# A fused sparse-attention and MLP kernel: a shorter start chain, a seventh tracked PSUM bank, and an order of work taken from a search of the scheduling model

## The chip, the cores and the metric

The kernel runs on one core of a Trainium2 chip. The metric is the device time of one execution in microseconds (us). Most executions of one kernel agree within a few tenths of a per cent, some kernels here only within about one per cent, and medians are quoted. PSUM is the memory that matmuls write to, in eight banks here. PE is the matrix engine, PEld its weight loads, DVE the vector engine, ACT the scalar engine, POOL the general one, SP the engine that issues most DMA transfers here.

## The reference, cut to what matters

Block-sparse attention over 4 batches, 8 heads, 768 positions and a head size of 64, followed by a residual MLP of two steps, one across positions ("token" work) and one across channels:

```python
mask = |qb - kb| <= 1, or first / last block, or one of 3 sampled blocks per query block
attn = softmax(where(mask, q k^T / 8, -1e9)) v          # B=4, H=8, S=768, D=64
x    = attn rearranged to [B, 768, 512]
tok  = w_tok @ (alpha1 * x + beta1)                      # 768 x 768 over positions
u    = x + lam * tok
a2   = alpha2 * u + beta2
out  = u + lam * (relu(a2 @ w_ch1) @ w_ch2)              # 512 -> 2048 -> 512
```

Sixteen pairs of heads are worked off one after another. The first channel product (`uT`, `w1b`) fills a bank of PSUM, ACT or DVE applies the relu and writes a slice of the tile `hts`, and the second channel product (`w2b`, `hts`) reads four such slices at a time.

## The kernel before

The program has no fixed loop nest. It holds a list of jobs (engine, modelled duration, priority, buffers taken and given) and a model of the chip's time. The model walks through time, picks the next job for each engine, and so writes one fixed instruction order for every engine. The chip then runs that order. Where the model finds nothing for PE to do it puts in dummy matmuls (`fill`), which are instructions like any other: if the chip is later than the model, PE still has to run them. The parts that the change and the argument touch:

```python
def bank_order(tc, instructions, psum, nb):
    # for every instruction that touches the shared PSUM tile: which waits it really needs
    ...
        for kind in ("ins", "outs"):
            for a in getattr(ins, kind):
                ...
                if ap.tensor.name != psum:
                    names.add(ap.tensor.name)        # any other tile: by its name, as a whole
                    continue
                ...                                  # the shared PSUM tile: bank by bank
        if not banks:
            continue                                 # touches no bank: left to the usual tracking
        ...
        for n in names:
            for r in shared.get(n, ()):              # every earlier instruction that named it
                if r.engine != ins.engine or ins.engine != mybir.EngineType.PE:
                    real[r.name] = r                 # keep a dependency on it
            shared.setdefault(n, []).append(ins)
        tc.declare_no_dep(ins, group=psum, keep=list(real.values()), reason="other banks")
```

```python
ps6 = ps.tile([P, 6 * 512], FP, name="ps6", ...)     # six banks in one tile, handled by bank_order
BANKS = tuple(f"b{i}" for i in range(6))
...
wps = ps.tile([P, 512], FP, name="cp", tag="cp", bufs=1)   # a tile of its own: dummies and w2b products
keep_warm(9, 512)                                    # nine dummies before any data is there
...
# second channel product: into "cp" or "ops", both tiles of their own
cps[kk, mi] = bank(tag, [P, DM]) if tag in BANKS else ps.tile([P, DM], FP, name=tag, tag=tag, bufs=1)
for nk in range(4 * r, 4 * r + 4):
    nc.tensor.matmul(cps[kk, mi][:, 0:w], hts[kk][:, nk, ts(m, P)], w2tile[0][:, nk, lo : lo + w], ...)
...
T0 = 6600.0                                          # the model's time at which the list starts
```

The softmax here doesn't subtract the row's maximum and nothing guards it: scores larger than these inputs give would overflow.

## Time and profile before

| | before |
|---|---|
| time, median of 3 runs | 310.68 us (310.44 to 310.88) |
| span of the profiled execution | 308.2 us |
| first scores / first channel matmul / first `w2b` matmul | 7.72 / 59.70 / 72.05 us |
| last matmul | 304.45 us |
| clock of PE released | 6.4 us after the start |

The prediction below shows the main views. The waits of PE over the whole span (engine, line, what it waited for, then total us, times, longest) are two:

```profile
PE cp L236 <- DVE warm L231: 1.2, 1, 1.2
PE ps L716 <- ACT qx L303: 0.7, 1, 0.7
```

Both lie in the start. After it PE never waits long enough to be listed. The waits of ACT begin with the relu L1039:

```profile
ACT hts L1039 <- PE ps L1026: 36.4, 26, 9.6
```

In the timeline of SP's issues (start, length, kind) the mask goes out before any transpose of a head:

```profile
46.47 15.78 SPq L556 DMA_DIRECT2D maskT<-mask_rows  x18
62.55 1.32 SPq L657 DMA_TRANSPOSE qx<-rel  x1
```

### The profile page before, as it was taken

The numbers are of one execution on the slowest core, as the hardware profiler recorded it, in microseconds if no ns is written. First come the engines' busy times: TensorE is split into PE (matmuls) and PEld (weight loads), VectorE is DVE, ScalarE is ACT, GpSimd is POOL, SyncE is SP. The second block draws the span as 40 slices with busy tenths as digits, with TensorE's granted clock in tenths as the row PEclk, the third lists the DMA queues.
The fourth block names the chain that finished last, engine by engine and source line by source line (L and its number), as shares of the span: only waits on it lengthen the run. The fifth ranks groups of instructions, "written<-read, shape, count | busy, mean of one in ns | idle before, by whom it ended". The sixth has DMA issues, their size and how long they took to land.

```text
span 308.2 us, 7605 instructions
## 1 busy us (share of the span) xinstructions
PE 302.7 (98%) x3197; PEld 189.0 (61%) x3197; DVE 207.6 (67%) x434; ACT 206.3 (67%) x272; POOL 53.2 (17%) x91
## 2 busy tenths in 40 slices
PE   7999999999999999999999999999999999999995
PEld 3687788775656557555656557555656665555444
DVE  3699898879979788778759788778768730010111
ACT  4999998988676667577676666577658727428000
POOL 4656532001121121212021121120000000000000
PEclk9999999999999999999999999999999999999999
DMA  6999999993347634874444624983110110010121
GB/s 150 186 258 224 212 203 215 177 146 68 51 101 123 104 62 54 146 121 95 76 93 84 102 62 56 147 107 79 28 37 34 28 28 34 34 70 0 50 89 68
DMA packets 47210, 30.81 MB, mean 100 GB/s; under 512 B 27552, under 2 KB 43080, under 8 KB 47176
## 3 DMA queue, kind: packets, MB, share of 16 engines
q0 software_dynamic: 15984, 15.47, 32.0%
q1 hardware_dynamic: 30940, 14.61, 21.0%
q8 instruction: 25, 0.41, 0.6%
q10 hardware_dynamic: 252, 0.24, 0.2%
q14 instruction: 9, 0.07, 0.1%
HBM read 32.04 MB, written 6.33 MB: 124 GB/s over the span
## 4 chain that ended last, share of the span: by engine, by line
PE 76%; DMA 15%; issue 4%; POOL 3%; DVE 1%; POOLq 0%
PE ps L1026 26%; PE cp L1076 22%; DMA v<-in_v_dram 9%; PE ops L870 8%; PE ps L837 8%; PE ps L947 7%; PE ops L1076 5%; DMA k<-in_k_dram 3%; DMA wtk<-in_moe_w_tok_dram 3%; DMA q2f<-in_q_dram 1%; POOL q L383 1%; POOL k L383 1%; POOL w1b L448 1%; POOL v L383 0%; DVE x_sb L957 0%
## 5 line engine op out<-in xcount | busy, mean ns | idle before, releaser
L789 ACT ACTIVATE eT<-ps 128x1024 f16<-128x1024 f32 x90 | 87.0, 1023 | 29.4 <-PE ps L837 28.6
L1026 PE MATMUL ps<-uT,w1b 128*128 128x384 bf16 (+1 forms) x512 | 92.9, 326 | 0.1
L1039 ACT ACTIVATE hts<-ps,b1t 128x384 bf16<-128x384 f32 x106 | 61.4, 583 | 40.3 <-PE ps L1026 36.4
L1076 PE MATMUL cp<-w2b,hts 128*128 128x512 bf16 (+1 forms) x320 | 77.2, 374 | 0.0
L794 DVE TENSOR_TENSOR eT<-eT,maskT 128x1024 f16<-128x1024 f16 x90 | 60.6, 686 | 12.7 <-ACT eT L789 12.5
L1026 PEld LDWEIGHTS <-w1b 128*128 128x128 bf16 x512 | 46.9, 98 | 30.3 <-ACT eT L789 1.0
L1076 PEld LDWEIGHTS <-hts 128*128 128x128 bf16 x400 | 36.6, 98 | 36.4 <-issue 3.0
L731 ACT ACTIVATE eT<-ps 128x1024 f16<-128x1024 f32 (+1 forms) x55 | 52.4, 1020 | 3.4 <-PE ps L716 3.2
L870 PEld LDWEIGHTS <-eT 128*128 128x128 f16 x720 | 30.9, 97 | 15.7 <-issue 3.8
L947 PE MATMUL ps<-a1p,wtokT 128*128 128x128 bf16 x576 | 36.2, 219 | 0.0
L870 PE MATMUL ops<-vext,eT 128*128 128x65 f16 x720 | 35.8, 193 | 0.0
L947 PEld LDWEIGHTS <-wtokT 128*128 128x128 bf16 x576 | 32.9, 98 | 1.5 <-issue 0.6
L1093 DVE TENSOR_TENSOR ot<-x_sb,cp 128x512 f32<-128x512 f32 (+1 forms) x20 | 13.5, 673 | 28.4 <-PE cp L1076 28.3
L716 PE MATMUL ps<-qx,kx 88*128 88x512 bf16 (+1 forms) x144 | 31.7, 326 | 0.7 <-ACT qx L303 0.7
L381 POOL COPY held<-flag 1x1 bf16<-1x1 bf16 x24 | 10.5, 438 | 123.1 <-DVE flag L401 123.1
L837 PE MATMUL ps<-qx,kx 64*128 64x512 bf16 (+1 forms) x240 | 26.1, 326 | 0.0
L756 PEld LDWEIGHTS <-eT 128*128 128x128 f16 x432 | 18.2, 97 | 4.6 <-DVE x_sb L691 0.6
L756 PE MATMUL ops<-vext,eT 128*128 128x65 f16 x432 | 20.2, 193 | 0.0
L957 DVE TENSOR_TENSOR x_sb<-x_sb,ps 128x384 f32<-128x384 f32 x32 | 17.6, 550 | 3.5 <-PE ps L947 3.1
L691 DVE TENSOR_TENSOR x_sb<-ops,rcp 128x384 f32<-128x384 f32 x32 | 17.8, 558 | 1.1
L1093 DVE TENSOR_TENSOR ot<-x_sb,ops 128x512 f32<-128x512 f32 (+1 forms) x5 | 3.2, 635 | 22.5 <-PE ops L1076 22.5
L1043 DVE TENSOR_SCALAR hts<-ps,b1t 128x384 bf16<-128x384 f32 x22 | 13.6, 618 | 6.8 <-PE ps L1026 5.2
(69 smaller groups left out, 227.2 us busy)
## 6 DMA issues: line engine op xcount, KB each, us to landing
out_dram<-ot SPq DMA_DIRECT2D x23, 256.0 KB
v<-in_v_dram POOLq DMA_DIRECT2D x16, 192.0 KB, 4.4
q<-in_q_dram POOLq DMA_DIRECT2D x15, 192.0 KB, 4.7
k<-in_k_dram POOLq DMA_DIRECT2D x15, 192.0 KB, 3.5
w1b<-in_moe_w_ch_dram POOLq DMA_DIRECT2D x4, 512.0 KB, 9.9
w2b<-in_moe_w_ch_dram POOLq DMA_DIRECT2D x4, 512.0 KB, 15.0
wtk<-in_moe_w_tok_dram POOLq DMA_DIRECT2D x3, 384.0 KB, 9.6
maskT<-mask_rows SPq DMA_DIRECT2D x14, 72.0 KB
```

The costliest lines, as they stand in the source:

```text
L691: nc.vector.tensor_tensor(out=x_sb[:, s0 : s0 + NT, h * D : (h + 1) * D], in0=op[:, :, 0:D], in1=rcp[:].unsqueeze(2).broadcast_to([P, NT, D]),
L716: nc.tensor.matmul(sps[:, f - u * UN : f - u * UN + w], kx[h][0:KC, ts(jt, P)], qx[h][0:KC, c : c + w], start=True, stop=True,)
L731: nc.scalar.activation(eT[:, c], sps[:, c], AF.Exp, bias=EXPB, scale=SCALE)
L756: nc.tensor.matmul(ops[p, a][:, t * VW : t * VW + D + 1], eTs[p, u][:, ts(i - u * GU, P)], vx[:, a, jt, 0 : D + 1], start=(i % HT == 0), s ...
L789: nc.scalar.activation(eT[:], sps[:], AF.Exp, bias=EXPB, scale=SCALE)
L794: nc.vector.tensor_tensor(out=e, in0=e, in1=maskT[:, u, :].unsqueeze(1).broadcast_to([P, 2, 512]), op=ALU.min,)
L837: nc.tensor.matmul(sps[:, a * 512 + lo : a * 512 + lo + w], kx[sl][r, ts(jt, P)], qx[sl][r, c : c + w], start=True, stop=True,)
L870: nc.tensor.matmul(ops[p, a][:, t * VW : t * VW + D + 1], eTs[p, u][:, a * 512 + c * P : a * 512 + (c + 1) * P], vx[:, a, jt, 0 : D + 1], ...
L947: nc.tensor.matmul(tp[:, j, :], wtokT[:, s, ts(3 * g + j, P)], tl["a1p", p][:, s, :], start=(s == 0), stop=(s == NT - 1),)
L1026: nc.tensor.matmul(hp[:, 0:nc_], w1b[:, dk, ts(f, P)], uTs[b][:, dk, hf * HS : hf * HS + nc_], start=(dk == 0), stop=(dk == 3),)
L1039: nc.scalar.activation(hts[kk][:, f, :], hp[:, 0:HS], AF.Relu, bias=b1t[:, f : f + 1], scale=1.0)
L1076: nc.tensor.matmul(cps[kk, mi][:, 0:w], hts[kk][:, nk, ts(m, P)], w2tile[0][:, nk, lo : lo + w], start=(nk == 0), stop=(nk == 15),)
```

## The change

Its intent is to begin the scores a microsecond earlier, to give the order of work a seventh PSUM bank for single products, and to replace a hand-made order of loads and some priorities by one that a search found to be shorter in the scheduling model. Cut to its core:

```diff
-LEAD = 18
+LEADS = (14, 14, 14, 14, 29, 22, 28, 13, ...)        # one per pair
+PATS = (0.0, 0.0, 0.0, 0.0, 0.0, 1200.0, ...)        # how long a group waits for more units
+NUDGE = {(2, 26, 0): -3.0, ...}                       # priorities of five jobs
+LOADS = ("v 0", "q 1", "k 1", "a1", "tok 0", "k 2", "q 2", "q 4", "v 1", ...)
+PR = 0                                                # priority of DVE jobs of the fourth pair
+UTN = 3                                               # transposes of ub that leave PE for DMA
...
-    ps6 = ps.tile([P, 6 * 512], FP, name="ps6", tag="ps6", bufs=1)
+    ps6 = ps.tile([P, 7 * 512], FP, name="ps6", tag="ps6", bufs=1)
+    ALL = BANKS + ("b6",)              # b6 takes w2b products, dummies and some early scores
...
-    wps = ps.tile([P, 512], FP, name="cp", tag="cp", bufs=1)
-            nc.tensor.matmul(wps[:, 0:w], warm[:, 0:P], warm[:, 0:w], start=True, stop=True)
+            nc.tensor.matmul(bank(name, [P, w]), warm[:, 0:P], warm[:, 0:w], start=True, stop=True)
...
-    keep_warm(9, 512)
+    keep_warm(7, 512)
+    keep_warm(2, P)
...                                        # start chain: two small tables in one transfer, the mask
...                                        # product from kx[3], its scaling in the copies behind it
-    T0 = 6600.0
+T0 = 5600.0
...
-        if b == 0:
+        if b == 0 and n >= UTN:           # else: DMA transpose on SP
...
-                        cps[kk, mi] = bank(tag, [P, DM]) if tag in BANKS else ps.tile(...)
+                        cps[kk, mi] = bank(tag, [P, DM]) if tag in ALL else ps.tile(...)
...
-                take = ((("cp", "ops") + ...
+                take = ((("b6", "ops") + ...
...
-    bank_order(tc, list(nc.cur_bb.bb.instructions), ps6_name[0], len(BANKS))
+    bank_order(tc, list(nc.cur_bb.bb.instructions), ps6_name[0], len(ALL))
```

## The prediction

> **What bounds the kernel now.** I read the page's busy table first, then one table of five stretches of the span, then the order of instructions inside three of them.
>
> ```profile
> PE 302.7 (98%) x3197; PEld 189.0 (61%) x3197; DVE 207.6 (67%) x434; ACT 206.3 (67%) x272; POOL 53.2 (17%) x91
> ```
>
> PE (the matrix engine) is the bound, but 98% can't be taken as 98% useful: dummy matmuls on the tile `warm` keep it awake and count as busy. The stretches, chosen at the first scores (7.72), the first channel matmul of L1026 (59.70), the last token work and the last matmul (columns: length, then busy time and count on PE, weight loads, DVE, ACT, POOL, then clock, DMA share, GB/s):
>
> ```profile
> 0.00:7.72 7.72, 5.87 (x24) 2.47 (x25) 2.97 (x12) 3.21 (x5) 3.86 (x10) 1.00 0.64 150
> 7.72:59.70 51.98, 51.98 (x781) 40.40 (x782) 44.91 (x98) 49.36 (x55) 22.52 (x34) 1.00 1.18 213
> 59.70:254.50 194.80, 194.67 (x2114) 118.92 (x2113) 153.36 (x316) 135.14 (x181) 26.80 (x48) 1.00 0.48 82
> 254.50:304.45 49.95, 49.95 (x281) 27.21 (x278) 5.93 (x9) 18.59 (x32) 0.00 (x0) 1.00 0.13 48
> 304.45:308.20 3.75, 0.27 (x3) 0.00 (x0) 0.42 (x1) 0.00 (x0) 0.00 (x0) 0.81 0.17 57
> ```
>
> Five regimes. (1) 7.72 us before any score. (2) 52 us of attention: ACT is busy 49.36 of 51.98 with exps of about 1.03 us each, so ACT sets the pace and PE fills up with dummies. (3) 195 us in which attention and channel matmuls mix. (4) 50 us of channel matmuls alone. (5) A 3.75 us tail. In (3) and (4) PE never waits to speak of.
>
> The start-to-start distance of neighbouring matmuls says what PE really spends. Four channel matmuls take 0.65 us (L1026) or 0.86 us (L1076), 18 token matmuls 1.00 us. Around a group of paired scores (L837) there is more:
>
> ```profile
> 120.41 0.28 PE L870 MATMUL ops<-vext,eT 128*128 128x65 f16 x4
> 120.63 0.61 PE L837 MATMUL ps<-qx,kx 64*128 64x512 bf16 x6
> 121.17 1.04 PE L1076 MATMUL cp<-w2b,hts 128*128 128x512 bf16 x4
> ```
>
> The four L870 take 4 x 0.029 = 0.12 us, so L837 could start at 120.53 and starts at 120.63; its six matmuls run two at a time and need 2 x 0.216 = 0.43 us, and the next starts at 121.17, not 121.06. Over all 38 such groups I find 0.20 us a group, the same for groups of two units and of three: 38 x 0.204 = 7.8 us. Other distances above the usual sum to 0.3 us after 59.7. So the end is first scores + real PE work + dummies + group changes + tail; nothing else has room.
>
> The first scores hang on this chain:
>
> ```profile
> 1.19 4.02 PE L236 MATMUL cp<-warm 128*128 128x512 bf16 x9 [1.19 <-DVE warm L231]
> 2.60 1.28 ACT L277 ACT_TABLE_LOAD   x1 [2.60 <-issue]
> 3.89 0.51 ACT L277 CAST rel<-k2f 128x384 bf16<-128x384 f32 x1
> 5.01 0.85 PE L284 MATMUL ps<-identb,rel 128*128 128x128 bf16 x6
> 5.79 0.49 PE L294 MATMUL ps<-kx,mbb 24*24 24x384 bf16 x1
> 6.31 0.36 DVE L298 COPY kx<-ps 64x384 bf16<-64x384 bf16 x1 [1.20 <-PE ps L294]
> 7.21 0.47 ACT L303 CAST qx<-ops 24x384 bf16<-24x384 f32 x1
> 7.72 1.03 PE L716 MATMUL ps<-qx,kx 88*128 88x512 bf16 x5 [0.66 <-ACT qx L303]
> ```
>
> Two avoidable waits stand in it. The cast of k is over at 4.40, but nine cold dummies (0.427 us start to start) keep PE until 5.01. And the DVE copy into `kx` idles 1.20 us for L294, which reads other rows of the same tile.
>
> **What the Trainium skill says.** *Perfetto Trace Analysis*, Identifying the Most-Contended Engine, calls matmul busy share a poor measure of distance to the limit; this trace agrees, as PE is shown 98% busy with 11.4 us of dummies in it. *TensorE: Matmul & The Clock Gate*, What's actually happening, says that the array starts at half rate and is released after some 3.4 us of activity; here 128-column matmuls are 0.107 us apart at 5.0 to 5.5 us and 0.056 us apart from 6.56 us. *TensorEngine Tiling (Array Packing)*, Key Properties, says that a change of tiling mode drains the engine; the 0.20 us around each L837 group (64 rows against 128) fits, though other causes are not excluded. *DMA: Bandwidth & Descriptors*, DMA Transpose (X-bar), says the plain transpose is issued by Sync or ScalarE alone; the twelve transposes of `uT` on SP agree.
>
> **The change, part by part.**
> *Start.* Seven wide and two narrow dummies instead of nine: 7 x 0.427 + 2 x 0.107 = 3.20 us from 1.19, so PE is free at 4.39. One ACT-queue issue fewer (the 0.66 us `tab`) lets the table load and the cast of k go earlier; that cast then waits for k itself, which I put at 3.65, and ends at about 4.15. Transposes start at 4.4 instead of 5.01: -0.6 us. The mask product reads `kx[3]`, so the DVE copy no longer waits for it; the 0.38 us L261 goes, its arithmetic moving into the two copies that follow the product anyway. Walking on with the old durations: transposes to 5.05, products at 5.1 and 5.4, DVE copies to about 6.1, its mask rows to 6.7; ACT's mask rows by 6.4, and the last ACT copy (upper half of `kx`) is not needed by the first unit. First scores at about 6.75: **-0.95 us**.
>
> *Dummies and transposes in stage 2.* By the built order, dummies after the first scores go from 10,422 to 12,659 columns: at 2.4 columns a ns, 4.34 to 5.27 us, **+0.93 us**. Three of four batch-0 transposes of `ub` leave PE for DMA: 18 x 0.056 = **-1.0 us**. The two cancel; the first channel matmul comes again at the 48th unit of attention, as before. So stage 2 keeps its length of 52 us and only starts earlier. ACT has one 0.8 us copy fewer in it, but that can't help: the dummies are fixed instructions, and PE has to run them.
>
> *Groups.* The lead limits, the patience and the seventh bank change how paired scores are grouped: 24 of two units and 14 of three become 15 and 20. 38 to 35 groups: 3 x 0.204 = **-0.6 us**.
>
> *Rest.* All other matmuls keep their number and shape. Attention now ends nearer to the end (in the built order some 48 us of PE work follows the last token matmul, before 57), still enough to hide everything. The tail of 3.75 us stays.
>
> Sum: -0.95 + 0.93 - 1.0 - 0.6 = -1.6 us, from 310.7 to **309.1 us**.
>
> **The rivals.**
> A. *The order of loads misfits the chip.* Stage 2 moves 213 GB/s at a DMA share above 1, and the loads wait in one POOL queue. In the new order two of the `w1` slices come very late, after the v of five pairs, and three DMA transposes join the crowd. Order on PE is fixed, so a late load stops it. For it: the list was found in a model, not on the chip. Against: the old `w1` loads were issued by 28 us and needed at 59.7. Cost if true: 1 to 3 us, giving 310 to 312.
> B. *The mask becomes the wait.* On SP the third `uT` transpose now stands ahead of the 15.8 us of mask issues, which started at 46.5 and had the head transposes right behind them until 69.6. If that transpose waits until 51, the first paired scores move to about 74. The built order has moved them behind the first L1076 work, where I put 74; a miss costs 1 to 2 us.
> C. *The early start is swallowed*, because loads, not scores, pace stage 2: then only 0.5 us is won, 310.1. Against it: ACT runs its first sixteen exps with no gap.
> D. *The start and priorities are worth more*: if the three high-priority token steps of the fourth pair arrive early, PE still can't skip its dummies; the most I see is 1 us more, 308.
>
> **Range and chances.** The three gains are counted on the engine that is never idle, so I hold on to 309.1; a few tenths of error each way on the start, and A or B one time in four. Range 307.9 to 310.8. A gain over 2% needs 6.2 us, more than all the waits I can find outside the start; a loss over 2% needs a stall of 7 us. Faster 0.03, same 0.95, slower 0.02.
>
> **What would show it.** First scores at 6.6 to 7.0 us; first channel matmul at 58.2 to 59.2; 35 groups of paired scores at 0.20 us each; the last matmul at about 302.8, with the tail unchanged. The prediction is wrong if PE shows idle time or stretched matmul distances between 40 and 80 us (A by a wait for `w1b`, `v` or `uT`, B by one for `maskT`, `qx` or `kx`), or if the clock is released late because the shorter warm-up leaves a gap.

## More of the kernel before

Whatever an instruction reads outside the shared tile is known to `bank_order` only by name. The relu reads a bank of `ps6` and writes `hts`, so it is handled there. The second channel product wrote `cp`, so it was not.

## The result, and the profile after

The changed kernel is correct and slower: 320.73 us median of 4 runs (318.06 to 321.22), against 310.78 us for the kernel before in the same rounds. The ratio is 1.0304, with a 95% interval of 1.0245 to 1.0362. Ratios here and below are the mean time of one kernel's fast runs over that of the other's of the same rounds, so not quite the ratio of the medians quoted.

From the page after, the busy line and the clock line (tenths of full speed in 40 slices):

```profile
PE 308.4 (97%) x3185; PEld 190.9 (60%) x3185; DVE 206.0 (64%) x429; ACT 207.1 (65%) x273; POOL 53.3 (17%) x91
PEclk9999999799999999999999999999999999999999
```

Twelve matmuls fewer than before (18 transposes fewer, six dummies more), and yet 5.7 us more of busy time. Part of that is dummies, and part ran on a slower clock: the 7 in the eighth slice (56 to 64 us) shows it. The table by stage, cut at first scores, first channel matmul, first `w2b` matmul and last matmul (length, then busy time and count of PE, PEld, DVE, ACT, POOL, then clock, DMA share, GB/s):

```profile
0.00:7.54 7.54, 5.78 (x24) 2.70 (x25) 2.81 (x12) 3.22 (x5) 3.56 (x10) 1.00 0.63 152
7.54:66.92 59.38, 56.55 (x769) 41.87 (x769) 43.84 (x98) 48.88 (x54) 22.64 (x34) 0.97 1.15 195
66.92:85.27 18.35, 17.13 (x186) 11.50 (x184) 13.82 (x31) 13.18 (x26) 0.00 (x0) 1.00 0.54 110
85.27:315.80 230.53, 228.67 (x2207) 134.82 (x2208) 145.12 (x291) 141.78 (x189) 27.08 (x48) 1.00 0.40 71
```

The second stage took 59.38 us where it took 51.98 before, so the first channel matmul came 7.2 us late. The last two stages together took 248.88 us where 244.75 us stood before, another 4.1. PE has idle time in all of them now.

To see what the time went into, I split the start-to-start distances of all matmuls into useful work (at the usual distance for their width), dummies, and the rest, which holds waits, group changes and the slow clock:

| us | first scores | to first channel matmul: work, dummies, rest | from there to the last matmul: work, dummies, rest | last matmul |
|---|---|---|---|---|
| before | 7.72 | 46.39, 4.73, 0.86 | 235.52, 0, 9.22 | 304.45 |
| after | 7.54 | 45.39, 6.61, 7.38 | 235.53, 0, 13.36 | 315.80 |

So of 11.35 us, 0.18 was won in the start and 1.0 in transposes. Dummies took 1.9 more, the rest before the first channel matmul (waits and the slow clock) 6.5, and the rest after it 4.1. Three places carry it.

**The start.** PE's timeline:

```profile
1.19 3.38 PE L246 MATMUL ps<-warm 128*128 128x512 bf16 x9 [1.19 <-DVE warm L242]
4.94 0.80 PE L288 MATMUL ps<-identb,rel 128*128 128x128 bf16 x6 [0.36 <-DMA identb<-ident_c]
...
7.54 1.86 PE L723 MATMUL ps<-qx,kx 88*128 88x512 bf16 x5 [0.21 <-ACT kx L312]
```

The dummies end early as planned, but the identity for the transposes lands only at 4.94, so they start when they did before and there is a gap of 0.36 us. The first scores ran cold: five of them took 1.86 us against 1.03 before, and the clock was released at 13.0 us, not 6.4.

**The middle of stage 2.** SP's issues, then DVE's and PE's timelines there, then one piece of the chain that ended last:

```profile
43.33 7.26 SPq L1002 DMA_TRANSPOSE uT<-ub  x2
...
55.16 1.23 SPq L1002 DMA_TRANSPOSE uT<-ub  x1
60.04 13.37 SPq L563 DMA_DIRECT2D maskT<-mask_rows  x18
```

```profile
49.25 0.55 DVE L943 TENSOR_TENSOR a1p<-a1p,b_bc 128x384 bf16<-128x384 bf16 x1
53.14 0.56 DVE L971 TENSOR_TENSOR ub<-x_sb,a_bc 128x384 bf16<-128x384 f32 x1 [3.34 <-DMA uT<-ub]
```

```profile
52.81 0.61 PE L723 MATMUL ps<-qx,kx 88*128 88x512 bf16 x3
56.16 0.51 PE L288 MATMUL ps<-identb,rel 128*128 128x128 bf16 x6 [2.73 <-DVE rel L578]
```

```profile
43.33 9.79 DMA uT<-ub
```

Read backwards: PE stood 2.73 us for a cast by DVE (`rel`). DVE had stood 3.34 us for a buffer of `ub`, of which there are two. The buffer was being read by a DMA transpose issued at 43.33 that took 9.79 us to land. After PE's wait the clock fell to half from 57.4 to 60.8 us.

**The channel work.** The waits of PE over the span, and the first line and the new line of ACT's:

```profile
PE ps L288 <- DVE rel L578: 2.7, 1, 2.7
PE ps L1084 <- DVE hts L1051: 1.6, 2, 1.0
...
PE ps L1084 <- ACT hts L1047: 0.7, 1, 0.7
PE ps L844 <- ACT hts L1047: 0.6, 2, 0.4
```

```profile
ACT hts L1047 <- PE ps L1034: 28.4, 29, 11.8
...
ACT hts L1047 <- PE ps L1084: 4.4, 4, 1.1
```

Before, the relu (L1039 then, L1047 now) waited for the product that it reads and for nothing else that lasted. Now it also waits for the `w2b` product L1084, and L1084 waits for relus. One such place, PE and then ACT:

```profile
222.66 1.02 PE L1084 MATMUL ps<-w2b,hts 128*128 128x512 bf16 x4
224.35 1.02 PE L1084 MATMUL ps<-w2b,hts 128*128 128x512 bf16 x4 [0.67 <-ACT hts L1047]
```

```profile
223.72 0.58 ACT L1047 ACTIVATE hts<-ps,b1t 128x384 bf16<-128x384 f32 x1 [1.11 <-PE ps L1084]
```

ACT holds its relu back until the first four `w2b` matmuls are done at about 223.7, although the slice of `hts` that it writes is read only by the next four, which wait for it in turn. The two engines take turns where they should overlap.

### The profile page after: what moved, and what is told of

Read it like the earlier page. It is cut to its first block, busy times and chain, and to the rows that moved or that the text cites. A ratio compares the mean times of both kernels' runs of the same rounds, so it can differ in the third digit from the quotient of the medians.

```text
span 319.4 us, 7587 instructions
## 1 busy us (share of the span) xinstructions
PE 308.4 (97%) x3185; PEld 190.9 (60%) x3185; DVE 206.0 (64%) x429; ACT 207.1 (65%) x273; POOL 53.3 (17%) x91
## 4 chain that ended last, share of the span: by engine, by line
PE 90%; DMA 4%; ACT 2%; DVE 2%; issue 0%; SPq 0%; ACTq 0%
PE ps L1034 25%; PE ps L1084 23%; PE ps L955 9%; PE ops L877 8%; PE ps L844 7%; PE ps L723 7%; PE ops L1084 4%; PE ops L763 4%; DMA uT<-ub 3%; ACT hts L1047 2%; PE ps L246 2%; PE ps L288 2%; DMA identb<-ident_c 1%; DVE hts L1051 1%; PE ps L500 1%
## 5 line engine op out<-in xcount | busy, mean ns | idle before, releaser
L1047 ACT ACTIVATE hts<-ps,b1t 128x384 bf16<-128x384 f32 x107 | 62.1, 581 | 37.8 <-PE ps L1034 28.4
L1084 PE MATMUL ps<-w2b,hts 128*128 128x512 bf16 (+1 forms) x336 | 80.1, 374 | 2.3 <-DVE hts L1051 1.6
L801 DVE TENSOR_TENSOR eT<-eT,maskT 128x1024 f16<-128x1024 f16 x90 | 60.8, 686 | 25.8 <-ACT eT L796 25.6
L1084 PEld LDWEIGHTS <-hts 128*128 128x128 bf16 x400 | 36.2, 97 | 37.6 <-issue 3.7
L877 PEld LDWEIGHTS <-eT 128*128 128x128 f16 x720 | 30.5, 97 | 14.9 <-issue 3.6
L955 PE MATMUL ps<-a1p,wtokT 128*128 128x128 bf16 x576 | 37.3, 220 | 0.0
L1101 DVE TENSOR_TENSOR ot<-x_sb,ps 128x512 f32<-128x512 f32 (+1 forms) x21 | 14.1, 671 | 34.5 <-PE ps L1084 34.3
L955 PEld LDWEIGHTS <-wtokT 128*128 128x128 bf16 x576 | 34.0, 99 | 2.8 <-issue 0.3
L877 PE MATMUL ops<-vext,eT 128*128 128x65 f16 x720 | 35.2, 193 | 0.0
L723 PE MATMUL ps<-qx,kx 88*128 88x512 bf16 (+1 forms) x144 | 33.3, 342 | 0.2 <-ACT kx L312 0.2
L763 PEld LDWEIGHTS <-eT 128*128 128x128 f16 x432 | 17.7, 99 | 4.4 <-DVE x_sb L698 0.4
L971 DVE TENSOR_TENSOR ub<-x_sb,a_bc 128x384 bf16<-128x384 f32 x32 | 17.4, 553 | 3.6 <-DMA uT<-ub 3.3
L763 PE MATMUL ops<-vext,eT 128*128 128x65 f16 x432 | 19.0, 195 | 0.0
L844 PEld LDWEIGHTS <-kx 64*128 64x128 bf16 x240 | 8.9, 94 | 14.6 <-issue 6.6
```

The costliest lines, as they stand in the source:

```text
L723: nc.tensor.matmul(sps[:, f - u * UN : f - u * UN + w], kx[h][0:KC, ts(jt, P)], qx[h][0:KC, c : c + w], start=True, stop=True,)
L763: nc.tensor.matmul(ops[p, a][:, t * VW : t * VW + D + 1], eTs[p, u][:, ts(i - u * GU, P)], vx[:, a, jt, 0 : D + 1], start=(i % HT == 0), s ...
L801: nc.vector.tensor_tensor(out=e, in0=e, in1=maskT[:, u, :].unsqueeze(1).broadcast_to([P, 2, 512]), op=ALU.min,)
L844: nc.tensor.matmul(sps[:, a * 512 + lo : a * 512 + lo + w], kx[sl][r, ts(jt, P)], qx[sl][r, c : c + w], start=True, stop=True,)
L877: nc.tensor.matmul(ops[p, a][:, t * VW : t * VW + D + 1], eTs[p, u][:, a * 512 + c * P : a * 512 + (c + 1) * P], vx[:, a, jt, 0 : D + 1], ...
L955: nc.tensor.matmul(tp[:, j, :], wtokT[:, s, ts(3 * g + j, P)], tl["a1p", p][:, s, :], start=(s == 0), stop=(s == NT - 1),)
```

## The experiments

Sixteen runs, in four batches on one chip each; the kernel before ran in the same rounds, with medians of 310.89, 311.36, 310.99 and 310.78 us. "First scores" and the like are from each run's own profile.

### Batch 1: the parts of stage 2 and of the start

**e1_ub3**, a third buffer for the tile that the DMA transposes read; the instruction order stays identical.

```diff
-                    tl["ub", p] = wk.tile([P, NT, P], BF, name="ub", tag="ub", bufs=2)
+                    tl["ub", p] = wk.tile([P, NT, P], BF, name="ub", tag="ub", bufs=3)
```

> The changed kernel with a third buffer for ub and every instruction in the same order. Theory D (the three batch-0 transposes that went to DMA land after 10 us, and DVE stops for the ub buffer that the first of them holds): the 3.3 us wait of DVE on ub goes, the 2.7 us wait of PE on the cast of k goes, the clock does not drop at 57 us, and the first channel matmul moves from 66.9 to 62 or 63 us; time 316 to 317.5 against 320.7. Rival L (late loads are what delays stage 2): DVE and PE wait as long at the same place for q or k, first channel matmul within 1 us of 66.9, time within 1 us of 320.

319.29 us, ratio 1.0268 (1.0234 to 1.0302), some 1.4 us below the changed kernel and outside the range expected. DVE's wait of 3.34 us went, PE's wait for `rel` went, and no clock drop followed. The first channel matmul still came at 62.41 and not at 59.70: there are 1.8 us more of dummies than before and 2.0 us more of rest, most of it the clock, released only at 12.9 us, less the 1.0 us of transposes. And two matmuls later, from 62.9 to 65.2 us, PE stands for the third DMA transpose itself, which was issued at 51.73 and took 13.38 us to land:

```profile
PE ps L1034 <- DMA uT<-ub: 2.3, 1, 2.3
```

The late DMA transposes are real, but freeing the buffer is worth far less than the 7 us by which stage 2 was late, and a wait for the transpose takes its place.

**e2_9wide**, the nine wide dummies of before.

```diff
-    keep_warm(7, 512)
-    keep_warm(2, P)
+    keep_warm(9, 512)
```

> The changed kernel with the nine wide dummies of before at the start, all else in the same order. Theory C (the idle 0.36 us of PE between the shortened dummies and the late identity put off the release of the clock from 6.4 to 13.0 us): release back near 6.4 us, the ACT waits of about 2.5 us between 9 and 14 us go, the 20th exp of ACT starts 1.5 to 2.5 us earlier, time 1 to 2.5 us shorter. Rival P (the moment of the release is chance[...]): release anywhere from 6 to 13 us whatever the dummies, no clear difference of the medians.

318.49 us, ratio 1.0233 (1.0192 to 1.0273), 2.2 below the changed kernel. The first execution, the profiled one, ran slow as a whole (520 us at a recorded clock of 0.56), so there is no usable trace, and when its clock was released is not known; the other three agree.

**e3_utn0**, all transposes of `ub` of the first batch back on PE. The model then chooses a somewhat different order.

```diff
-UTN = 3
+UTN = 0
```

> The changed kernel with all four batch-0 transposes of ub on PE as before, which the scheduler orders anew. Theory D: no wait of DVE on ub, no clock drop near 57 us, first channel matmul at 60 to 62 us, time 313 to 316. Rival L: first channel matmul stays later than 65 us, time above 318.

321.3 us, ratio 1.031 (1.0255 to 1.0365): no gain, where 313 to 316 was expected. Its clock was released at 13.5 us. One of its four runs took 318.53 against 321.2 to 321.5, as one of the changed kernel's took 318.06 against 320.3 to 321.2.

**e4_utn0_9wide**, both edits together.

> Both undone: transposes on PE and nine wide dummies. If D and C are all that went wrong in stage 2: first channel matmul at 59 to 60 us, time 310.5 to 313, the rest being waits after 80 us that the changed kernel has and before lacks (about 3 to 4 us). If it stays above 315, something else in stage 2 is at work.

318.91 us, ratio 1.0254 (1.0223 to 1.0284). Beside e3 only the dummies differ: the clock was released at 7.2 instead of 13.5 us, the first channel matmul came 2.0 us earlier (62.85 against 64.88), and the median fell by 2.4 us. With e2 this sizes the late clock, in these orders, at 2.2 to 2.4 us. Over all traces in the fast state, the ten with nine wide dummies have the clock free by 7.2 us; the five with short ones at 13.0 (changed kernel), 12.9 (e1), 13.5 (e3), 9.7 (e10) and 4.6 (e13). So short dummies risk a late release and don't force it. The gap behind them does not decide: beyond the usual distance of the matmuls it is 0.22 us in e3 and 0.19 in e13, which are the latest and the earliest of the five. What does decide is not shown. With 318.9 for the 310.5 to 313 that was expected, most of the loss was still unexplained after batch 1.

### Batch 2: the searched order

**e5_old_order**, e4 with the old order of loads, one lead limit of 18, no patience, no nudges, the old priorities and T0 = 6600. The order of instructions after the start is then that of the kernel before.

```diff
-LEADS = (14, 14, 14, 14, 29, ...)     # and PATS, NUDGE, LOADS, PR
+LEADS = (18,) * 16                    # PATS all 0.0, NUDGE {}, old LOADS, PR = 2
-T0 = 5600.0
+T0 = 6600.0
```

> The changed kernel with nine wide dummies, all transposes of ub on PE, and the old list of loads, leads, patience and start time of the model: its order after the start is that of the kernel before, instruction by instruction. So only the new chain to the first scores and the seventh bank are left of the change. Theory O (the loss is in the order and the dummies, the start and the bank do no harm): 310.2 to 311.0, same as before, first channel matmul within 0.4 us of 59.7. Rival B (the seventh bank, shared in one tile, brings new waits): 1 us or more above before, with waits on the bank that before lacks.

316.68 us, ratio 1.0168 (1.0135 to 1.0201). This was the turning point. The order was that of before, the start was shorter, and yet 5.3 us were lost. What still differed was where the `w2b` products go. I then listed the waits of the built programs: in this one 24 of the 128 relus wait for a `w2b` matmul, before it was 19. Counted more sharply, by the last matmul that the semaphore wait of a relu names in the built program, it is a `w2b` matmul for 11 relus here, for 5 in the changed kernel and for none before. (Its profiled execution ran slow as a whole, 1,095 us, so its trace could not tell.)

**e6_T0_early**, e5 with T0 = 5600 alone.

```diff
-T0 = 6600.0
+T0 = 5600.0
```

> The same as the run with the old order, but the model starts its engines at 5.6 us as in the change and not at 6.6. In the built order 5.85 us of dummies stand before the first channel matmul instead of 4.40, and 47.3 us of work instead of 46.4. Theory T (the model starts 1 us too early against the real first scores, and so the order it makes misfits): first channel matmul 2 to 4 us later than 59.7, time 1.5 to 4 us longer than the old order. Rival: the start time only shifts everything, under 0.5 us.

322.66 us, ratio 1.0362 (1.0324 to 1.04), 6.0 us above e5 from one constant. Its first paired scores wait for a head's DMA transpose:

```profile
PE ps L843 <- DMA kx<-rel: 3.4, 1, 3.4
```

A model that believes to start 1 us earlier does not shift the same order by 1 us. It picks another order, and this one does not fit the chip.

**e7_old_leads**, e4 with the old LEADS, PATS and NUDGE; **e8_old_loads**, e4 with the old LOADS.

```diff
-LEADS = (14, 14, 14, 14, 29, ...)     # e7; PATS and NUDGE too
+LEADS = (18,) * 16
```

```diff
-LOADS = ("v 0", "q 1", "k 1", "a1", "tok 0", ...)    # e8
+LOADS = ("v 0", "q 1", "k 1", "v 1", "q 2", ...)     # the order of before
```

> The changed kernel with transposes of ub on PE and nine wide dummies, and with the old lead limit of 18, no patience and no nudges; loads stay in the new order. Against the run with the same but the new leads (318.9, whose waits and group changes from the first w2b matmul to the end sum to 14.4 us, 8.6 before). Theory W (the new leads and patience place w2b matmuls right behind the relus they need and score groups before their banks are free): that sum falls to 8.5 to 10.5 us and the time to 313.5 to 316. Rival: the sum stays above 13 us.

> The changed kernel with transposes of ub on PE and nine wide dummies, and with the old order of loads; the new leads stay. In the built order it has 7.1 us of dummies before the first channel matmul, more than the new loads with 5.8. Theory L (new order of loads starves stage 2): first channel matmul earlier than 62.0, time 1 us or more below 318.9. Theory W: first channel matmul at 62 to 64, no gain, and waits after it as with the new loads.

e7: 317.2 us, ratio 1.0187 (1.0145 to 1.0228), 1.7 below e4. I had held that the new leads made the waits after the first `w2b` matmul; that fell, since the rest in that stage stayed above 14 us. e8: 330.7 us, ratio 1.0602 (1.0557 to 1.0647), the worst of all. So the old order of loads does not go with the new leads and T0 = 5600; the searched list is better for the settings it was searched with. (Its profiled execution was slow as a whole too, 449 us.)

### Batch 3: finer tracking

The next theory was that the seventh bank brought the waits: `w2b` products now touch the shared tile, so `bank_order` handles them, and it knows `hts` only as a whole. The edit makes it compare the ranges that two instructions touch:

```diff
-                if ap.tensor.name != psum:
-                    names.add(ap.tensor.name)
-                    continue
-                step = a.ap[0][0]
+                step = a.ap[0][0] or 1 << 40
                 lo = ap.offset % step
                 hi = lo + sum((n - 1) * s for s, n in list(a.ap)[1:])
+                if ap.tensor.name != psum:
+                    names.add((ap.tensor.name, lo, hi, kind))
+                    continue
...
-        for n in names:
-            for r in shared.get(n, ()):
+        for n, lo, hi, kind in names:
+            for r, l2, h2, k2 in shared.get(n, ()):
+                if l2 > hi or h2 < lo or kind == k2 == "ins":
+                    continue
```

**e9_old_order_fine** is e5 with it, **e10_after_fine** the changed kernel with it, **e11_after_fine_9_ub3** the changed kernel with it, nine wide dummies and the third `ub` buffer.

> The run with the old order (316.7, before 311.4), where now dependencies between the instructions that touch the shared PSUM tile are drawn only where the parts of hts they read and write overlap, and not for the whole tile. In the built program relus that wait for a w2b matmul fall from 24 to 19, the number of before. Theory F (w2b products moved into the shared tile, and so into a tracking that takes hts as a whole: relus wait for w2b matmuls that read other parts, w2b matmuls for relus they do not need): 310.3 to 311.5, the 5 us are back. Rival (the new chain to the first scores costs it): stays above 315.

> The changed kernel with the finer tracking of hts and nothing else changed. Theory F: the waits of PE on hts after the first w2b matmul (3.5 us in its profile) go, and 3 to 4.5 us of 320.7: 316 to 318. Rival (leads and patience make those waits, F only in the old order): less than 1 us gained.

> The changed kernel in its own order with three repairs: finer tracking of hts, nine wide dummies, a third buffer for ub. If the causes add up: 320.7 less 3.5 (tracking), 2.2 (clock), 1.5 (ub) = 313.5, within 312.5 to 314.5. What is left above 311 is then the landing of the transposes (first channel matmul at 60 to 61 us and a wait on uT behind it) and the dummies.

e9: 312.14 us, ratio 1.0037 (0.9993 to 1.0081), 4.5 below e5 and just above its range. e10: 314.54 us, ratio 1.0099 (1.0045 to 1.0153), 6.2 below the changed kernel, more than expected, and no wait for `hts` is left in PE's list. From the first channel matmul to the last it takes 243.9 us, 5.0 less than the changed kernel in the same order; the rest was won ahead of it, where the clock was released at 9.7 us.

e11: 313.27 us, ratio 1.0052 (1.0005 to 1.01). It hit its range by luck, for its sum was wrong: the tracking alone had already won 6.2 us and not 3.5, and the dummies and the buffer added 1.3 and not 3.7. The first channel matmul came at 59.76, as before, but then PE waits 2.0 us for `uT` and the clock falls to half from 63.4 to 66.9 us.

**e12_best**, e9 with a patience of 1200 and leads of 22 throughout, which makes 33 groups of paired scores instead of 38: the try for a kernel that beats both.

```diff
-LEADS = (18,) * 16
-PATS = (0.0,) * 16
+LEADS = (22,) * 16
+PATS = (1200.0,) * 16
```

> A candidate to beat before: the run with the old order and finer tracking, with a patience of 1.2 us everywhere and a lead of 22, which makes 33 groups of paired scores of 38. By 0.20 us a group 1.0 us under before: 309.6 to 310.5. If patience makes PE idle instead, 311 or more.

310.72 us, ratio 0.9982 (0.9945 to 1.0018): the same as before, not better. It has first scores at 6.44 us and five groups fewer, and gives both back, for the most part while PE waits for token results on DVE (which had itself waited for loads, as batch 4 shows):

```profile
PE ps L1035 <- DVE x_sb L966: 2.0, 2, 1.7
```

### Batch 4: the seventh bank alone

Finer tracking changes two things at once, the waits that the seventh bank made and false waits elsewhere, above all in the start. Two questions were therefore open: which of the two won the 6 us, and whether the DMA transposes hold the rest.

**e13_after_cp** is the changed kernel with bank b6 as a tile of its own again, tracking as coarse as ever. **e14_old_order_cp** is e5 with the same edit. In both the built order on all five engines is identical, instruction for instruction, to that of the kernel they start from; only the waits differ.

```diff
-    ps6 = ps.tile([P, 7 * 512], FP, name="ps6", tag="ps6", bufs=1)
+    ps6 = ps.tile([P, 6 * 512], FP, name="ps6", tag="ps6", bufs=1)
+    cpt = ps.tile([P, 512], FP, name="cp", tag="cp", bufs=1)
...
-        t = ps6[:, ts(ALL.index(name), 512)]
+        t = cpt[:, 0:512] if name == "b6" else ps6[:, ts(ALL.index(name), 512)]
...
-    bank_order(tc, ..., ps6_name[0], len(ALL))
+    bank_order(tc, ..., ps6_name[0], len(BANKS))
```

> The changed kernel with its seventh bank as a tile of its own again, and the tracker otherwise as coarse as before; the order on all five engines is the changed kernel's, instruction for instruction. Bank theory: the waits of PE for hts after the first channel matmul (4.4 us above those of before) go, the late start of stage 2 and the late clock stay: 316 to 317.5 us, first scores still near 7.5 us. Rival (the finer tracking won its 6.2 us by freeing the start or other tiles): no change, 320 to 321.

> The run with the old order of work (316.7) with the seventh bank as a tile of its own again and coarse tracking; order identical to that run. Bank theory: some 4.5 us less, 312 to 312.8. Rival (gain of the finer tracking lay elsewhere): 316 to 317.

e13: 315.48 us, ratio 1.0151 (1.0093 to 1.0208), 5.2 us below the changed kernel. e14: 310.99 us, ratio 0.9994 (0.9956 to 1.0033), 5.7 us below e5 and level with the kernel before. Both are somewhat below what the bank theory asked for, and far from the rival. The waits of PE in e13:

```profile
PE ps L289 <- DVE rel L579: 3.7, 3, 2.2
PE cp L247 <- DVE warm L243: 1.2, 1, 1.2
PE ps L724 <- ACT kx L313: 0.6, 1, 0.6
PE ps L501 <- DMA wtk<-in_moe_w_tok_dram: 0.4, 1, 0.4
PE ps L1035 <- DVE hts L1052: 0.2, 1, 0.2
```

Those of `w2b` products and of paired scores for `hts` are gone, and so is ACT's wait for the `w2b` product; in the built programs of e13 and e14 no relu's wait names a `w2b` matmul last, as before. The wait of stage 2 for `rel` is still there (2.2 us). The two other waits for `rel`, 0.3 us at 13.7 and 1.25 at 21.0, come from loads: DVE had stood 3.24 us for `k` and 1.15 for `q`. From the first channel matmul (65.11) to the last one (310.09) it is 244.98 us, against 244.75 before and 248.88 after. The last matmul came 5.7 us earlier than in the changed kernel's profile, and 3.9 of that lie here. The other 1.8 lie ahead, where in this execution the identity was there in time and the clock was released at 4.6 us. So the trace gives the bank 3.9 us in this order. The median of 5.2 may hold some luck of the start: the five runs fall into 314.3 to 315.5 and 317.5 to 317.6, the four of the changed kernel into 318.06 and 320.3 to 321.2, and group against group the difference is 3.2 to 3.4 us. What makes the two groups is not shown. At the place shown above neither engine waits for the other any more.

In e14 the first scores and the first channel matmul (59.33) came 0.4 us earlier than before. The gain is lost at 68.7 us, where PE waits 1.5 us for a token result on DVE, and DVE's cast of `k`, which stands ahead of it in DVE's order, waits for a load. Before and e14:

```profile
66.99 0.36 DVE L571 COPY rel<-k 128x768 bf16<-128x768 bf16 x1 [0.72 <-DMA k<-in_k_dram]
68.52 0.36 DVE L578 COPY rel<-k 128x768 bf16<-128x768 bf16 x1 [1.90 <-DMA k<-in_k_dram]
```

Between 62 and 72 us DVE stands 1.2 us for loads of q, k and v before, and 2.6 in e14, 2.3 in e15, 3.6 in e9 and 3.2 in e12; PE then waits 1.5, 1.3, 2.4 and 2.0 us for the token results. An earlier start does not help while these loads land no earlier.

**e15_before_fine**, the kernel before with the finer tracking alone, and **e16_after_fine_9_utn0**, the changed kernel with finer tracking, nine wide dummies and UTN = 0. Their edits are those shown above.

> The kernel before with the finer tracking alone. Its w2b products are in a tile of their own, so the bank theory leaves it little: only what the start gains, first scores up to 1 us earlier, 309.7 to 311. Rival (coarse tracking costs every kernel 4 to 6 us): 305 to 307.

> The changed kernel with finer tracking, nine wide dummies and all batch-0 transposes of ub on PE. If the late DMA transposes cost what the waits show (2.0 us for uT, against 1.0 us of PE work saved), it is 0.5 to 1.5 us below the run with the third ub buffer (313.3): 312 to 312.8. If the rest is the misfit of the order with the chip, it stays at 313 to 314.

e15: 311.01 us, ratio 0.9985 (0.995 to 1.0021): coarse tracking cost the kernel before nothing, because its `w2b` products were never in the tracked tile. e16: 312.63 us, ratio 1.0043 (1.0005 to 1.008), inside the range for the transposes' theory, but not apart from e11 (1.0052), which keeps the DMA transposes behind a third buffer. The two ran on different chips and in different orders, and e11 pays its 2.0 us wait for `uT` where e16 pays 0.4 us more dummies and 1.0 us of transposes. So these runs show no measurable difference between PE and DMA for these transposes once nothing waits for the buffer.

### The sum

Going from the changed kernel back to before by runs that differ in one group of edits each:

| step | median us | step |
|---|---|---|
| changed kernel | 320.73 | |
| e4: transposes on PE, nine wide dummies | 318.91 | -1.8 |
| e5: also the old order of work and T0 | 316.68 | -2.2 |
| e14: also bank b6 as a tile of its own | 310.99 | -5.7 |
| before | 310.78 | -0.2 |

What e14 still has of the change is the shorter start chain, and it is worth nothing at the end. The steps before the last don't add up in any order, as e6 and e8 show; that of the bank was measured twice, from different orders, as 5.2 and 5.7 us by the medians, and as 3.9 us in the trace of e13. The medians come from different batches, in which the kernel before moved by up to 0.6 us.

## Why the prediction was wrong

Predicted 309.1 us with same at 0.95; measured 320.7, slower. The views were read correctly as far as they went: PE is the bound, stage 2 and the channel work set the end, and the tail stayed (3.6 us after the last matmul, against 3.75). What failed is the sum itself: "nothing else has room" was read off the kernel before and carried over, so no term was left for waits. Waits and the slow clock are what grew, by 6.5 us before the first channel matmul and 4.1 after it (the rest in the table above), of 11.35 us in all. The steps:

- **Start, -0.95: mis-sized.** First scores came at 7.54, not 6.75. The step put the transposes at 4.4 because it followed the cast of k and the dummies, and left out the transfer of the identity, which landed at 4.94. It also held that the upper half of `kx` "is not needed by the first unit"; in the trace L723 waits for just that copy (0.21 us, and 0.61 us in e13). The scores don't need it, the bookkeeping does: with finer tracking (e11) the first scores wait for `qx` instead. What was gained was then swallowed, as **rival C** had it, and for its reason, loads: e14 reaches its first scores 0.36 us earlier and ends where before ends, and e9 and e12, with first scores at 6.44, gain nothing either. The place was another in e14, behind stage 2, where DVE waits for q, k and v at 65 to 70 us; in e13, with the clock released early, it was in stage 2, where loads of `k` and `q` held DVE.
- **"The clock is released late because the shorter warm-up leaves a gap"** stood only among the things that would make the prediction wrong. The late release happened, at 13.0 us, and cost 2.2 to 2.4 us by e2 and by e3 against e4. That it came from the gap is not shown (e3 and e13 speak against it). It got no term and no chance of its own.
- **Dummies +0.93 and transposes -1.0 cancel: this step failed.** The counts were right for the work (46.39 to 45.39 us), but "so stage 2 keeps its length of 52 us" assumed that nothing waits. It took 59.38. A transpose that leaves PE does not become free: here it held one of two `ub` buffers for 9.79 us, DVE stood 3.34 us, PE 2.73, and 3.4 us at half clock followed. The dummies measured 6.61 us instead of 5.66 (4.73 + 0.93), part of them on the slow clock.
- **Rival A** named the crowd of loads and DMA transposes, "a wait for `w1b`, `v` or `uT`", with one chance in four together with B and a cost of 1 to 3 us. It came true by `uT`, not by `w1b`, and in another form: PE did not wait for `uT`, but DVE did for the buffer that a transpose into `uT` was reading. Size: e1 takes back 1.4 us. **Rival B**: the mask did go out late (60.04 to 73.4, from 46.5 to 62.3 before) and the first paired scores fell to 86.24, but PE does not wait for it; by then the built order had moved them behind the first `w2b` work, itself late. **Rival D** did not occur.
- **Groups 38 to 35, -0.6: right in number, wrong in price.** The 15 groups of two cost 0.203 us each as before, but the 20 groups of three cost 0.26, as the matmul behind each came later: 15 x 0.203 + 20 x 0.26 = 8.3 us, against 38 x 0.204 = 7.8. So +0.5 instead of -0.6. With the bank in its own tile (e13) those of three are at 0.21, with finer tracking (e10) at 0.204, so the price belonged to the same false waits.
- **"All other matmuls keep their number and shape": the step that failed most.** It was true, and it was the wrong question. I compared instruction orders and never asked which waits each instruction would carry. The seventh bank was booked under grouping of scores only. In fact it moved the `w2b` products into a tile whose dependencies are worked out by a function that knows `hts` as a whole, so relus wait for `w2b` products and `w2b` products for relus. Shown by e13 and e14: same order, bank in its own tile, 5.2 and 5.7 us less by the medians, of which e13's trace puts 3.9 after the first channel matmul. The finer tracking (e10), which leaves the bank where it is, takes back 5.0 us there.

What stays open: how much of the 2.2 us between e4 and e5 belongs to the loads, the leads or T0 by themselves, since they only work together; why the loads behind the wait at 68 us land 1 us and more later in some profiles of nearly the same program than in that of before, which is about as large as the differences among the best kernels; and what decides when the clock is released.

## What to carry to other kernels

When a buffer moves into a tile that has its own dependency bookkeeping, everything that the instruction reads and writes falls under that bookkeeping too: compare the waits of the two built programs, not only the order of their instructions. An order found in a model is only good for the state of the chip that the model assumed; check the modelled latencies of what it moves (here DMA transposes under load) against the trace before trusting it. An earlier start is worth little while a load further on lands no earlier. And moving work off the bound engine needs a buffer for as long as the slower path really takes.

## What the Trainium skill lacked or had wrong

- *DMA: Bandwidth & Descriptors*, Latency and other measured facts, gives a DMA transpose an effective bandwidth of 261 GB/s in one kernel, and no landing time. Three transposes of 128 x 768 bf16 (196,608 bytes) issued while the core moved 195 to 201 GB/s landed 9.7 to 10.1 us after issue here, some 20 GB/s each; the next one, issued at 76.92 while it moved 97 GB/s, landed after 2.75 us.
- *TensorE: Matmul & The Clock Gate*, What's actually happening, has the clock drop after an idle window of about 3.4 us. Here it dropped after shorter waits of PE, of 2.73 us (changed kernel), 2.19 us (e13) and 1.98 us (e11), each time for some 3.4 us, and did not drop after one of 2.26 us (e1). Its release within some 3.4 us of activity fits the 4.6 us of e13, but in the changed kernel and e3, with PE at work from 1.19 us and no gap over 0.6 us, it came at 13.0 and 13.5 us.
- *Perfetto Trace Analysis*, Matmul Optimizations, advises to use all eight PSUM banks, and *PSUM — Partial Sum Buffer*, PSUM bank collisions raise a hardware error, to guard PSUM by bank and quadrant. Neither warns that the other operands of a tracked instruction must be tracked as finely: with the eight banks in use before and after, 3.9 us (trace of e13) to 5.7 us (e14) hung on that alone.
- *TensorEngine Tiling (Array Packing)*, Key Properties, says that a mode switch drains the engine, without a size. Around a group of 64-row scores it is 0.10 us in and 0.11 us out where nothing else waits.
- No page of those read here describes executions that are slow as a whole: the first executions of e2, e5 and e8 took 520, 1,095 and 449 us with recorded clocks of 0.56, 1.0 and 0.67, and the next ones of the same kernels 318, 317 and 329.
